# Moving the V gathers from GpSimd's queue to SyncE's, and a second buffer for attention output

## Chip, cores, metric

One core of one Trainium2 chip. The metric is device time in microseconds (us), the median of several executions. "State" says whether a run was fast or more than 1.5% above the fastest run of the same kernel (slow); verdicts use fast runs alone.

## The reference

Two branches share a layer-normalised input `xn` of 2048 tokens by 512 and are added to the input.

```python
# A: 32 heads of 16; each token looks at 8 keys, itself and those 2, 4 .. 14 tokens back
q, k, v = split(xn @ wqkv)
logits = einsum('bhsd,bhswd->bhsw', q, k_gathered) * scale     # masked where the index is < 0
o = einsum('bhsw,bhswd->bhsd', softmax(logits), v_gathered) @ wo
# B: gated MLP with mixing over tokens
z = gelu(xn @ w_in); z1 = z[:896]; z2 = layernorm(z[896:])
g = einsum('ts,bsf->btf', w_sp, z2) + b_sp                     # w_sp is 2048 x 2048
out = x + o + (z1 * g) @ w_out
```

## The kernel before

A small planner records every operation with what it reads and writes, estimates durations, fixes an order for each engine, and sets semaphore waits. For TensorE (PE) it keeps the order of the program. After projections and normalisation (to about 108 us) come four waves, tc = 0 to 3, of 512 tokens each. Each needs a transposed quarter of the spatial weights (2 MB in bf16, by transposing DMA, into one of two slots), and V rows for the attention sums, which VectorE (DVE) computes in two pairs, par = 0 and 1. I call the weight transposes wT0 to wT3 and the pairs (tc, par).

```python
def ld_wT(tc):                      # weights of wave tc; slot tc % 2; SyncE (SP)
    return dma("sp", lambda e: e.dma_start_transpose(AC(WT[tc % 2], [[512, NB], [1, 512]]),
                                                     B_w_sp[512 * tc: 512 * tc + 512, :]), ...)

def ld_V(j, par):                   # V gather: 128 rows of 9216 B from a scratch in HBM; GpSimd (POOL)
    src = bass.AP(tensor=vscr.tensor, offset=..., ap=[[1024, 128], [1, 4608]])
    dma("pool", lambda e: e.dma_start(A("Ve", 4608, 4608 * par), src), ..., writes=[("Ve", par)])

def pv_pair(j, par):                # DVE: two products of 4096, then sums a, b, c; the last into On
    ...
    return dma("sp", lambda e: e.dma_start_transpose(OT_of(j, par), A("On", 1024)), ...)  # attention transpose
# ... (cut)
for tc in range(NJ):
    # ... PE: products of the wave, with plain passes of the next one and output of the last between them
    for par in range(2):
        if tc > 0:
            ld_V(tc, par)
        sp_seq.append(pv_pair(tc, par))             # sp_seq: SP issues these in this order
        if par == 1 and tc + 2 < NJ:
            sp_seq.append(ld_wT(tc + 2))
```

Of the kernel before, what the change touches and what calls it, by code (L numbers as in the profile page):

```python
# [324 lines left out]
def build_kernel(nc, A_x, A_wqkv, A_wo, B_x, B_w_in, B_w_sp, B_b_sp, B_w_out, out, report=False, sched_kw=None,  # L325
# [3 lines left out]
    D = A_x.shape[2]  # L329
    assert D == 512 and S % 512 == 0  # L330
    NB = S // 128
    NJ = S // 512
# [5 lines left out]
    FILL = cfg["fill"]  # L338
# [8 lines left out]
    vscr = nc.dram_tensor("vscr", (2 * VPR, 512), BF).ap()  # L347
# [12 lines left out]
    off = {}  # L360
# [38 lines left out]
    with ExitStack() as es:  # L399
# [12 lines left out]
        def A(name, n, o2_=0):  # L412
            return ar[:, off[name] + o2_: off[name] + o2_ + n]
# [4 lines left out]
        def AC(o_, dims):  # L418
            return bass.AP(tensor=ar, offset=o_, ap=[[AR, 128]] + [list(d) for d in dims])
# [15 lines left out]
        def R1(key, name, n, o_=0):  # L435
            R(key, "sb", [(off[name] + o_, off[name] + o_ + n)])
# [26 lines left out]
            R1(("xn", s_), "xn", 512, 512 * s_)  # L463
            R1(("Vn", s_), "Vn", 512, 512 * s_)
        R1("Vs", "Vs", 4096)
        R1("On", "On", 1024)
        for s_ in range(2):
            R1(("Ve", s_), "Ve", 4608, 4608 * s_)
            for q in range(4):
# [47 lines left out]
        def c_dve(n, mode=1.0):  # L517
            return 155.0 + n / (0.96 * mode)
# [3 lines left out]
        def T(eng, fn, **kw):  # L522
            t = plan.add(eng, fn, **kw)
            if eng == "pe" and not t.name.startswith(("warm", "fill", "xTr", "red")):
                pe_seq.append(t)
            return t

        def dma(eng, fn, nbytes, chan, reads=(), writes=(), name="", xbar=False, prio=None):
            d = dict(chan=chan, nbytes=nbytes, xbar=xbar)
            if xbar:  # L530
                d["iss"] = 7700.0 if nbytes > 1000000 else 1200.0
            return T(eng, fn, reads=tuple(reads), writes=tuple(writes), name=name, prio=prio, dma=d)
# [9 lines left out]
          name="steps0")  # L542
        T("dve", lambda v: v.memset(FCa(foff["st6"] + 8, [[9, NB], [1, 1]]), LN_EPS * D), writes=["st_eps"], est=160,
          name="steps1")
# [4 lines left out]
          writes=["ident"], est=350, name="ident1")  # L549
# [5 lines left out]
          writes=[("KTpad", c, 0) for c in range(4)], est=200, name="ktpad", prio=2)  # L555
# [61 lines left out]
        for which, eng in ((0, "sp"), (1, "act")):  # L617
# [4 lines left out]
                name="ld%s" % ("qk"[which]))  # L622
# [329 lines left out]
        def bdiff(tc):  # L952
            T("dve", lambda v: v.tensor_tensor(bdt[:, 0:256], A("bbc", 256, 512 * tc + 256),
                                               A("bbc", 256, 512 * tc), ALU.subtract),
              reads=["bbc"], writes=["bd"], est=c_dve(256), name="bd%d" % tc)
# [73 lines left out]
        def plain_slices(tc, bank_of, cuts=(4, 4, 4, 4), fc=FC - 1):  # L1029
            r_ = tc % 2  # L1030
            st = {}

            def part(c0, c1):
                if c0 == 0:
                    st["k"] = bank_of()
                    cp(bank(st["k"]), A("bbc", 512, 512 * tc), ["bbc"], [("ps", st["k"])], 512, "gs%d_%d" % (fc, tc))
                k = st["k"]

                def mm(t):
                    last = None  # L1040
                    for sh in range(c0, c1):
                        last = t.matmul(bank(k), AC(off["z2"] + FH * sh + 128 * fc, [[1, 128]]),  # L1042
                                        AC(WT[r_] + sh * 512, [[1, 512]]), start=False, stop=(sh == NB - 1),
                                        skip_group_check=True)
                    return last
                T("pe", mm, reads=[(("z2a", "z2b", "z2c")[fc // 3], b) for b in range(c0, c1)] + [("wB", r_, q) for q in range(4)],
                  writes=[("ps", k)], est=(c1 - c0) * c_mm(512), name="gp%d_%d_%d" % (fc, tc, c0))
                if c1 < NB:
                    return
                sl = n_cb[0] % 2  # L1050
                n_cb[0] += 1
                cv = A("cb", 512, 1024 * sl)
                cp(cv, bank(k), [("ps", k)], [("cb", sl)], 512, "ge%d_%d" % (fc, tc))
                uv = AC(off["z1T"] + fc * S + 512 * tc, [[1, 512]])
                T("dve", lambda v: v.tensor_tensor(uv, cv, uv, ALU.mult), reads=[("cb", sl)], writes=[("z1T", fc, tc)],
                  est=c_dve(512, 2.0) + 30, name="up%d_%d" % (fc, tc))
            res = []
            c0 = 0
            for n in cuts:
                res.append((n, (lambda c0, n: lambda: part(c0, c0 + n))(c0, n)))  # L1060
                c0 += n
            return res
# [58 lines left out]
        def ld_V(j, par):  # L1121
            src = bass.AP(tensor=vscr.tensor, offset=vscr.offset + (VPR * par + 256 * j + 1) * 512,
                          ap=[[1024, 128], [1, 4608]])
            dma("pool", lambda e: e.dma_start(A("Ve", 4608, 4608 * par), src),  # L1124
                128 * 4608 * 2, ("Ve", par), reads=[("vscr", i) for i in range(4 * j - 1, 4 * j + 4)],
                writes=[("Ve", par)], name="ldVe%d_%d" % (j, par), prio=FILL)

        def pv_pair(j, par):
            v0 = off["Ve"] + 4608 * par
            for q in (par, par + 2):  # L1130
                b = 4 * j + q
                iv = AC(v0 + (7 + q // 2) * 512, [[-512, 8], [32, 16], [1, 32]])
                tv = iv if q >= 2 else AC(off["Vs"], [[512, 8], [32, 16], [1, 32]])
                av = AC(off["attn"] + 256 * b, [[32, 8], [0, 16], [1, 32]])
                T("dve", (lambda tv, iv, av: lambda v: v.tensor_tensor(tv, iv, av, ALU.mult))(tv, iv, av),  # L1135
                  reads=[("attn", j)] + ([("Ve", par)] if q < 2 else []),
                  writes=["Vs"] if q < 2 else [("Ve", par)], est=c_dve(4096, 2.0), name="pv%d" % b, prio=FILL)
            st_ = v0 + 512 - off["Vs"]

            def two(o_, n):  # L1140
                return AC(off["Vs"] + o_, [[st_, 2], [1, n]])
            for n, nm in ((2048, "a"), (1024, "b"), (512, "c")):
                o_ = two(0, n) if n > 512 else AC(off["On"], [[512, 2], [1, 512]])
                T("dve", (lambda o_, n: lambda v: v.tensor_tensor(o_, two(0, n), two(n, n), ALU.add))(o_, n),  # L1144
                  reads=[] if n > 512 else ["Vs", ("Ve", par)], writes=["Vs", ("Ve", par)] if n > 512 else ["On"],
                  est=c_dve(2 * n, 2.0), name="pv%s%d_%d" % (nm, j, par), prio=FILL)
            return dma("sp", lambda e: e.dma_start_transpose(AC(off["OT"] + 2048 * j + 1024 * par, [[128, 8], [1, 128]]),
                                                             A("On", 1024)),
                       128 * 1024 * 2, ("OTd", par), reads=["On"], writes=[("OT", 4 * j + par), ("OT", 4 * j + par + 2)],
                       name="OTd%d_%d" % (j, par), xbar=True)  # L1150

        n_out = [0]
# [73 lines left out]
        sp_seq = []  # L1226
# [8 lines left out]
        for tc in range(NJ):  # L1235
            if tc == 0 and P0:
                for fc in (3, 4, 5, 0, 1, 2, 6):
                    for n_, f_ in plain_slices(0, next_bank, (16,), fc):
                        f_()
                for n_, f_ in plain_slices(1, next_bank, (16,)):  # L1240
                    f_()
                for k0 in (0, 4):
                    s_sums(k0, k0 + 4, (1, 2, 4))
                    s_sums(k0, k0 + 4, (3,))
            else:
                q_ = []
                pl = plain_slices(tc + 1, ob) if tc + 1 < NJ else []
                oq = [out_slices(4 * (tc - 1) + q) for q in qord] if tc > 0 else [[], [], [], []]
                q_ = oq[0] + oq[1] + oq[2] + oq[3] + pl
                tot = sum(n for n, f in q_)  # L1250
                state = dict(done=0.0, gaps=0)

                def gap():
                    state["gaps"] += 1
                    while q_ and (state["done"] + 0.5 * q_[0][0] < tot * state["gaps"] / 9.0 or state["gaps"] == 9):
                        n, f = q_.pop(0)
                        f()
                        state["done"] += n
                for i in range(3):
                    prod7(i, tc, gap)  # L1260
                assert not q_
            for par in range(2):
                if tc > 0:
                    ld_V(tc, par)
                sp_seq.append(pv_pair(tc, par))
                if par == 1 and tc + 2 < NJ:
                    sp_seq.append(ld_wT(tc + 2))
            if tc + 1 < NJ:
                bdiff(tc + 1)
                t_sums(tc + 1)  # L1270
# [60 lines left out]
```

## Time and profile before

| | before |
|---|---|
| median of the runs known at the prediction | 259.72 us (259.46 to 263.94) |
| span of the profiled execution | 270.6 us |
| busy: PE, DVE, ACT (ScalarE), POOL | 239.3, 195.5, 142.6, 48.5 us |
| wT2, issue to landing | 47.4 us (of the four the shortest 10.1, the median 12.5) |
| V gather, issue to landing | 6.2 to 28.4 us, median 11.4 |

Landing means that a transfer's completion was signalled. The page's execution is a slow one by the rule above: its span alone is 4% above the fastest run (270.6 against 259.46 us). The waits on the page are longer than in an ordinary run. PE is the engine to watch: it is busy for 239.3 of the 270.6 us, so what costs time is what makes it idle, or halves its granted clock (0.50 from 162.4 to 169.2 us and from 172.7 to 189.6 us, 1.00 to 157.5 us). Its lines are shown in the prediction.

### The profile page before, as it was taken

To read this page: it belongs to the slowest core of one execution; us is meant where nothing else is said; L and a number is where in the kernel's file an instruction comes from. 1 tells how busy PE (TensorE), PEld (TensorE's weight loads), DVE (VectorE), ACT (ScalarE), POOL (GpSimd) and SP (SyncE) were. 2 spreads that over 40 slices of the span, in tenths; PEclk is the share of its full clock that TensorE was granted. 3 is DMA by queue.
4 is the path that set the end of the run, shared out by engine and by line. 5 is a ranking of instruction groups with operands and counts; after the bars stand their busy time and mean duration, and the time that the engine had idled before them with its cause. 6 is when DMAs were issued, how large, how long until landed. Compare 5 with 4: busy or idle time off the path is not lost.

```text
span 270.6 us, 3722 instructions
## 1 busy us (share of the span) xinstructions
PE 239.3 (88%) x1439; PEld 131.0 (48%) x1439; DVE 195.5 (72%) x228; ACT 142.6 (53%) x293; POOL 48.5 (18%) x82
## 2 busy tenths in 40 slices
PE   8999999999999999999999826005989998999994
PEld 2544434343453344444477614003767775777753
DVE  4687799899899899998994490004999999962020
ACT  2896669569899668671235303100345543545424
POOL 4648565760430400000000000000000000000000
PEclk9999999999999999999999995755999999999999
DMA  7969998320092490591099999998999663031112
GB/s 235 354 113 287 255 319 130 22 78 2 16 290 83 102 227 4 174 179 54 0 52 141 153 132 65 113 95 155 175 220 296 169 188 72 19 80 39 41 39 78
DMA packets 61697, 35.51 MB, mean 131 GB/s; under 512 B 49388, under 2 KB 60012, under 8 KB 60656
## 3 DMA queue, kind: packets, MB, share of 16 engines
q1 hardware_dynamic: 53600, 18.29, 42.5%
q0 software_dynamic: 1968, 11.55, 16.4%
q10 hardware_dynamic: 6112, 5.44, 8.9%
q8 instruction: 11, 0.18, 0.4%
q14 instruction: 6, 0.05, 0.1%
HBM read 19.01 MB, written 4.21 MB: 86 GB/s over the span
## 4 chain that ended last, share of the span: by engine, by line
PE 65%; DMA 15%; DVE 7%; SPq 6%; ACT 4%; ACTq 2%; issue 1%; POOL 0%; DVEq 0%
PE ps L1088 15%; PE ps L1042 11%; PE ps L1188 10%; PE ps L869 9%; PE ps L852 9%; DMA out_dram<-arena 8%; PE ps L729 5%; SPq L933 5%; PE ps L763 3%; PE ps L709 3%; DMA arena<-in_B_w_in_dram 2%; DMA arena<-in_B_b_sp_dram 2%; DVE arena L1135 2%; ACT arena L1015 1%; DVE arena L949 1%; DMA arena<-in_A_x_dram 1%
## 5 line engine op out<-in xcount | busy, mean ns | idle before, releaser
L1088 PE MATMUL ps<-arena 128*128 128x256 bf16 x504 | 62.6, 280 | 8.6 <-ACT ps L1015 8.6
L1088 PEld LDWEIGHTS ps<-arena 128*128 128x128 bf16 x504 | 50.5, 101 | 22.5 <-ACT ps L1015 9.9
L1144 DVE TENSOR_TENSOR arena<-arena 128x4096 bf16<-128x4096 bf16 (+2 forms) x24 | 33.6, 1401 | 31.1 <-DMA arena<-arena 30.6
L1015 ACT ACTIVATE arena<-ps 128x512 bf16<-128x512 f32 (+3 forms) x45 | 22.5, 501 | 54.2 <-PE ps L1042 19.1
L1042 PE MATMUL ps<-arena 128*128 128x512 bf16 x160 | 36.5, 385 | 16.1 <-DMA arena<-in_B_w_sp_dram 16.1
L1188 PE MATMUL ps<-arena 128*128 128x512 bf16 (+2 forms) x187 | 42.6, 371 | 1.1 <-DMA arena<-arena 1.1
L1135 DVE TENSOR_TENSOR arena<-arena 128x4096 bf16<-128x4096 bf16 x16 | 36.6, 2289 | 0.6
L755 DVE TENSOR_TENSOR arena<-arena 128x4096 bf16<-128x4096 bf16 x16 | 36.1, 2283 | 0.0
L1042 PEld LDWEIGHTS ps<-arena 128*128 128x128 bf16 x160 | 15.7, 99 | 34.8 <-issue 17.3
L729 PE MATMUL ps<-arena 128*128 128x512 bf16 x128 | 29.3, 380 | 0.0
L1188 PEld LDWEIGHTS ps<-arena 128*128 128x128 bf16 x187 | 19.6, 109 | 15.7 <-DMA arena<-arena 1.4
L852 PE MATMUL ps<-arena 128*128 128x448 bf16 x128 | 26.3, 353 | 0.4 <-DMA arena<-in_B_w_in_dram 0.3
L1124 POOL DMA_DIRECT2D arena<-vscr x8 | 4.4, 554 | 120.9 <-DVE arena L1144 118.8
L869 PE MATMUL ps<-arena 128*128 128x512 bf16 x112 | 25.0, 379 | 0.0
L1015 ACT ACTIVATE ps<-arena 128x512 f32<-128x512 bf16 (+3 forms) x36 | 19.0, 535 | 7.5 <-DMA arena<-in_A_x_dram 3.5
L737 ACT ACTIVATE arena<-ps 128x1024 bf16<-128x1024 f32 x16 | 16.3, 1019 | 7.9 <-PE ps L729 7.9
L857 ACT ACTIVATE arena<-ps 128x448 bf16<-128x448 f32 x32 | 17.2, 546 | 5.3 <-PE ps L852 3.8
L729 PEld LDWEIGHTS ps<-arena 128*128 128x128 bf16 x128 | 12.0, 98 | 16.1 <-issue 1.7
L874 ACT ACTIVATE arena<-ps 128x512 bf16<-128x512 f32 x28 | 15.8, 600 | 5.2 <-PE ps L869 5.0
L852 PEld LDWEIGHTS ps<-arena 128*128 128x128 bf16 x128 | 11.8, 98 | 13.6 <-issue 2.1
L1015 ACT ACTIVATE ps<-ps 128x256 f32<-128x256 f32 x27 | 9.9, 367 | 16.0 <-PE ps L1088 9.5
L1112 DVE TENSOR_TENSOR arena<-ps,wtt 128x512 bf16<-128x512 f32 x9 | 6.2, 687 | 15.8 <-ACT arena L1015 15.8
(67 smaller groups left out, 240.5 us busy)
## 6 DMA issues: line engine op xcount, KB each, us to landing
arena<-vscr POOLq DMA_DIRECT2D x8, 1152.0 KB, 11.4
arena<-in_A_x_dram ACTq DMA_DIRECT2D x18, 128.0 KB, 4.5
vscr<-arena POOLq DMA_DIRECT2D x16, 128.0 KB, 5.0
out_dram<-arena ACTq DMA_DIRECT2D x15, 128.0 KB, 3.0
arena<-in_A_x_dram SPq DMA_DIRECT2D x14, 128.0 KB, 6.8
arena<-in_A_wqkv_dram SPq DMA_DIRECT2D x2, 512.0 KB, 7.8
arena<-in_B_w_in_dram SPq DMA_DIRECT2D x1, 896.0 KB, 5.3
arena<-in_B_w_out_dram SPq DMA_DIRECT2D x1, 896.0 KB, 5.2
```

The source lines that it names most:

```text
L729: last = t.matmul(bank(k + which), AC(off["wqk"] + 1024 * dc + col0, [[1, 128]]), AC(off["xnT"] + dc * S + 512 * j, [[1, 512]]), start=(dc ...
L737: T("act", lambda a: a.activation(AC(qo, [[ko - qo, 2], [1, 512]]), ps[:, 512 * k: 512 * k + 1024].rearrange("p (t n) -> p t n", t=2), ACT ...
L755: T("dve", lambda v: v.tensor_tensor(pbv, qb, kb, ALU.mult), reads=rd, writes=[("pb", s_)], est=c_dve(4096, 2.0), name="prod%d_%d" % (j, c ...
L852: last = t.matmul(ps[:, 512 * k: 512 * k + HF], AC(off["xnT"] + dc * S + 128 * b, [[1, 128]]), AC(off["w_in2"] + FH * dc + c0, [[1, HF]]), ...
L857: T("act", (lambda k, hf: lambda a: a.activation(A("z2", HF, FH * b + HF * hf), ps[:, 512 * k: 512 * k + HF], ACTF.Gelu_apprx_tanh, accum_ ...
L869: lastm = t.matmul(bank(k), AC(off["w_in1"] + FH * dc + 128 * fc, [[1, 128]]), AC(off["xnT"] + dc * S + 512 * j, [[1, 512]]), start=(dc == ...
L1015: T("act", lambda a: a.activation(out_, in_, ACTF.Copy), reads=reads, writes=writes, est=c_act(n), name=name)
L1042: last = t.matmul(bank(k), AC(off["z2"] + FH * sh + 128 * fc, [[1, 128]]), AC(WT[r_] + sh * 512, [[1, 512]]), start=False, stop=(sh == NB ...
L1088: last = t.matmul(half(bk), lh(k), rh(k), start=False, stop=(k == NK - 1), skip_group_check=True)
L1135: T("dve", (lambda tv, iv, av: lambda v: v.tensor_tensor(tv, iv, av, ALU.mult))(tv, iv, av), reads=[("attn", j)] + ([("Ve", par)] if q < 2 ...
L1144: T("dve", (lambda o_, n: lambda v: v.tensor_tensor(o_, two(0, n), two(n, n), ALU.add))(o_, n), reads=[] if n > 512 else ["Vs", ("Ve", par ...
L1188: last = t.matmul(po, lh, rh, start=False, stop=(q == len(order) - 1), skip_group_check=True)
```

## The change

The intent is to take the gathers off GpSimd's software queue (q0 in the transfer tables), chain them on SyncE's hardware queue (q1) between the transposes, and let VectorE write one pair's sums while the other's transpose is still reading.

```diff
-        R1("On", "On", 1024)
+        R1(("On", 0), "On", 1024)
+        R1(("On", 1), "D", 1024)
@@ ld_V
-            dma("pool", ... name="ldVe%d_%d" % (j, par), prio=FILL)
+            return dma("sp", ... name="ldVe%d_%d" % (j, par))
@@ pv_pair
+            s_ = par if j else 0
+            on = off["D"] if s_ else off["On"]
... the last sum and its transpose use `on` and ("On", s_) instead of On
@@ waves
             for par in range(2):
-                if tc > 0:
-                    ld_V(tc, par)
                 sp_seq.append(pv_pair(tc, par))
+                if tc + 1 < NJ:
+                    sp_seq.append(ld_V(tc + 1, par))
```

More of the change, by code (lines that the diff above doesn't have):

```diff
@@ L1123, in ld_V @@
                           ap=[[1024, 128], [1, 4608]])
-            dma("pool", lambda e: e.dma_start(A("Ve", 4608, 4608 * par), src),
-                128 * 4608 * 2, ("Ve", par), reads=[("vscr", i) for i in range(4 * j - 1, 4 * j + 4)],
-                writes=[("Ve", par)], name="ldVe%d_%d" % (j, par), prio=FILL)
+            return dma("sp", lambda e: e.dma_start(A("Ve", 4608, 4608 * par), src),
+                       128 * 4608 * 2, ("Ve", par), reads=[("vscr", i) for i in range(4 * j - 1, 4 * j + 4)],
+                       writes=[("Ve", par)], name="ldVe%d_%d" % (j, par))
         def pv_pair(j, par):
             v0 = off["Ve"] + 4608 * par
+            s_ = par if j else 0
+            on = off["D"] if s_ else off["On"]
             for q in (par, par + 2):
@@ L1142, in pv_pair @@
             for n, nm in ((2048, "a"), (1024, "b"), (512, "c")):
-                o_ = two(0, n) if n > 512 else AC(off["On"], [[512, 2], [1, 512]])
+                o_ = two(0, n) if n > 512 else AC(on, [[512, 2], [1, 512]])
                 T("dve", (lambda o_, n: lambda v: v.tensor_tensor(o_, two(0, n), two(n, n), ALU.add))(o_, n),
-                  reads=[] if n > 512 else ["Vs", ("Ve", par)], writes=["Vs", ("Ve", par)] if n > 512 else ["On"],
+                  reads=[] if n > 512 else ["Vs", ("Ve", par)], writes=["Vs", ("Ve", par)] if n > 512 else [("On", s_)],
                   est=c_dve(2 * n, 2.0), name="pv%s%d_%d" % (nm, j, par), prio=FILL)
             return dma("sp", lambda e: e.dma_start_transpose(AC(off["OT"] + 2048 * j + 1024 * par, [[128, 8], [1, 128]]),
-                                                             A("On", 1024)),
-                       128 * 1024 * 2, ("OTd", par), reads=["On"], writes=[("OT", 4 * j + par), ("OT", 4 * j + par + 2)],
+                                                             AC(on, [[1, 1024]])),
+                       128 * 1024 * 2, ("OTd", par), reads=[("On", s_)], writes=[("OT", 4 * j + par), ("OT", 4 * j + par + 2)],
                        name="OTd%d_%d" % (j, par), xbar=True)
```

## The prediction

> **What bounds the kernel now.** I read the page's slices first, to see where the bounding engine falls idle, then the waits, to see what it waits for, then the timelines of the queues and the transfer table of the stretches concerned, to see why that comes late.
>
> ```profile
> PE   8999999999999999999999826005989998999994
> PEclk9999999999999999999999995755999999999999
> ```
>
> A slice is 6.77 us. TensorE (PE) is at eight or nine tenths in the first 22 slices and again in the last twelve, so it bounds the kernel everywhere except from about 150 to 190 us, where it falls idle and its granted clock drops to half. The waits name the reasons:
>
> ```profile
> DVE arena L1144 <- DMA arena<-arena: 30.6, 2, 23.4
> PE ps L1042 <- DMA arena<-in_B_w_sp_dram: 16.1, 1, 16.1
> ACT arena L1015 <- DMA out_dram<-arena: 11.1, 2, 10.6
> PE ps L1088 <- ACT ps L1015: 8.6, 3, 6.9
> ```
>
> The columns are total us, times, longest. PE waited 16.1 us for a spatial-weight transpose (the third, wT2), and 6.9 us for ACT, which itself had waited 10.6 us for an output store that had not landed. A third PE wait, 1.1 us, is for the transpose of the attention output. VectorE (DVE) waited 7.2 and 23.4 us for transposes of attention output to land, because the single buffer On can't be rewritten earlier. All three kinds are late transfers in one stretch. The timelines of SyncE (SP) and GpSimd (POOL) show what was in flight:
>
> ```profile
> 135.90 2.13 SPq L1147 DMA_TRANSPOSE arena<-arena  x1
> 138.07 44.62 SPq L933 DMA_TRANSPOSE arena<-in_B_w_sp_dram  x1
> 182.74 1.31 SPq L1147 DMA_TRANSPOSE arena<-arena  x1
> ...
> 136.18 0.55 POOL L1124 DMA_DIRECT2D arena<-vscr  x1 [21.09 <-DVE arena L1144]
> 153.63 0.53 POOL L1124 DMA_DIRECT2D arena<-vscr  x1 [16.91 <-DVE arena L1144]
> ```
>
> Columns: start, duration. SP needs 44.6 us merely to issue wT2; the first weight transpose took 7.58 us to issue. Beside wT2 run two V gathers of 1152 KB from POOL's queue; they landed after 16.2 and 28.4 us. The transfer table of two stretches (packets, MB, busy share of 16 engines), first the first weight transpose from 73 to 83 us, with no V gather beside it, then wT2 beside a gather from 165 to 179.9 us:
>
> ```profile
> DMA packets 8416, 2.62 MB, mean 262 GB/s; under 512 B 8288, under 2 KB 8288, under 8 KB 8416
> q1 hardware_dynamic: 8224, 2.10, 95.5%
> ...
> DMA packets 1658, 1.43 MB, mean 96 GB/s; under 512 B 1385, under 2 KB 1560, under 8 KB 1560
> q1 hardware_dynamic: 1351, 0.35, 77.9%
> q0 software_dynamic: 111, 0.90, 26.8%
> ```
>
> Alone, a transpose packet (2.10 MB / 8224 = 256 B) took 0.955*16*10 us / 8224 = 18.6 ns. Beside the gather it took 0.779*16*14.9 us / 1351 = 137 ns, and the total rate fell from 262 to 96 GB/s. A gather packet itself is cheap: the trace's DMA records have its 9216 B at 351 ns when nothing is mixed in, so 128 of them over 16 engines need 8*0.351 = 2.8 us. **Both** streams are slow at once, with the engines busy. So this isn't a shortage of bandwidth: the two queues disturb each other.
>
> [...] q0 and q1 advance together (the table above). [...] after 6.9 us and 16.1 us of idleness the stretch 157.5 to 191 has a mean granted clock of 0.64.
>
> **The change part by part.**
> *Queue.* The eight gathers leave POOL's queue q0 for SP's q1, ordered behind the attention-output transpose that precedes them and, for the next ones, before the weight transpose. Issue cost: 0.54 us each on POOL, about 0.6 us on SP (SP's 128 KB direct loads took 0.56 to 0.59 us), 4.8 us in all on an engine that is nearly always idle: nothing. [...] That same-queue neighbours don't hurt shows from 23 to 25 us, where the records have 256 B transposes at 18 ns in q1 beside plain loads of 1024 and 1792 B in q1, 337 GB/s together. After the change: attention-output transpose issued 135.9, gather 137.2, wT2 137.8; the gather takes 2.8 us, wT2 8192*18.6 ns/16 = 9.5 us,[...] some 2.5 us for ACT's stores and loads in q10 beside it (from 153 to 159 us wT2 beside q10 alone ran at 29 ns a packet, so 10 ns more on some 4000 packets / 16). So wT2 lands near 153 to 155 us instead of 185.5.
> *PE.* Without the 1.08 us and 6.88 us waits (the stores land in about 3 us in calm stretches) PE reaches the first matmul on wT2 at 157.5-1.1+2.6 = 159 us, where 2.6 us is the work at full clock that now lies from 164.4 to 169.5. wT2 is there by then, with some 4 us to spare. Removed: 1.08+6.88+16.06 = 24.0 us of idleness. With it goes the half clock: L1088 x16 and L1188 x4 took 3.59+1.52 against 1.75+0.86 us (2.5 us), and L1042 x4 with L1088 x24 took from 185.60 to 191.07, 5.5 us, against 0.86+2.62 (2.0 us). Sum 28.5 us.
> *Second buffer.* The sum of pair (j,1) for j>0 goes to the softmax area D, free by then. It removes the 23.4 us wait at 186.2 us directly. The first DVE wait, 7.2 us, is at j=1, par=0, still in On; it goes because its transpose is no longer mixed with a gather (landing 3 us instead of 16.7).
> *From page to time.* 270.6-28.5 = 242.1 us of span. But the page is of a bad execution: the run list has a core span of 257.4 us at clock 0.979 for a time of 259.1 us, close to the median 259.72. Check: half-clock time is 2*(1-0.956)*270.6 = 24 us in the page and 2*(1-0.979)*257.4 = 10.8 us there, so the ordinary stall is about half as long; 257.4-242.1 = 15.3 us can be removed in an ordinary run. With the 1.7 us between span and time: 242.1+1.7 = 243.8; I add 0.2 for small new waits and say **244.0 us**.
>
> **Rivals.** *A: the same 16 engines, nothing gained*[...]. Bytes don't change, so if packets of 9216 B hurt transposes from any ring the stall stays: 256 to 260 us. Against it: the two rates above[...]. *B: SP's chain holds the gathers up.* A gather may wait behind a weight transpose whose issue takes 7.6 to 10.3 us, and wT3 waits for PE to finish with the old weights, holding the next gathers. [...] Against: DVE reaches the pair (2,0) at about 156 us and its gather, behind wT2's issue, lands near 155; wT3 goes at about 166, so the gathers behind it start near 177 and DVE wants them at 183. A miss of some us in both places, passed to PE, makes 246 to 251. *C: DVE becomes the bound.* From 136 to the end DVE works 14.1+9.9+51.9 = 76 us and PE (at full clock) about 100, so no; but its order is chosen anew by the kernel's own scheduler, whose model now sees gathers on SP, and an unlucky order could cost 2 to 4 us. *D: the buffer alone does the work.* Then PE would still stand 16 us for wT2, and the time would stay above 256; the weight's lateness, not On, ends PE's wait.
>
> **Range and chances.** The floor is PE's work: busy 239.3 less 4.5 of half-clock excess, plus the 7 us of idleness at the start, the tail and small gaps, is the 242.1 of span again, so little below 242 is possible: low 241.5. Rivals B and C give the upper side: 251. A and D together get about one chance in fifteen; slower would need a new stall of over 20 us, for which I see no cause. Faster by over 2% (below 254.5): 0.93; within 2%: 0.06; slower: 0.01.
>
> **What would show it.** In the changed profile: the slices of PE without a gap near 150 to 190 us and a clock of 1.0 there; wT2's issue near 8 to 11 us and landing within 18 us; the waits for spatial weights and of DVE for attention transposes under 2 us each; the gathers in q1 with q0 left with the V writes only, and transpose packets near 20 ns. I'm wrong about the mixing if wT2 still takes over 25 us to land, and wrong about slack if PE waits for a gather's consumer (DVE waiting on vscr) by several us.

wT2's landing: from its issue 137.8 + 2.8 + 9.5 + 2.5 + 2.5 = 155.1 us. In the records of the kernel before, the first two weight transposes, with no gather beside them, took 2.9 and 1.8 us longer from issue to landing than their packets moved (11.2 against 8.3, 10.1 against 8.3).

## The result and the profile after

The changed kernel takes 244.14 us (243.27 to 246.3, 4 runs) against 261.83 us (259.46 to 268.09, 4 runs) before. The ratio is 0.9417, with a 95% interval of 0.9313 to 0.9521. Ratios here are the mean of one kernel's fast runs over the mean of the other's of the same rounds, so they aren't quite the ratios of the medians. The order of instructions on PE, DVE and ACT came out the same in both kernels; only SP's and POOL's lists differ. So the difference lies in the transfers and in what waits for them.

The slices of the changed kernel, of 6.06 us each now:

```profile
PE   7999999999999999999999999999699999999994
PEclk9999999999999999999999999999999999999999
```

PE's hole is gone, but for one slice at six tenths, and the granted clock never falls. Its waits in total, with times and the longest:

```profile
DVE arena L1138 <- DMA arena<-vscr: 3.2, 1, 3.2
...
PE ps L1089 <- ACT ps L1016: 2.5, 2, 2.0
```

PE's waits for weights (16.1 us) and attention transposes, and DVE's for attention transposes (30.6 us), no longer appear. What is left is one wait of DVE for a gather and a short one of PE. SP's timeline from the same stretch as before:

```profile
135.81 2.00 SPq L1150 DMA_TRANSPOSE arena<-arena  x1
137.85 0.58 SPq L1125 DMA_DIRECT2D arena<-vscr  x1
138.48 12.41 SPq L934 DMA_TRANSPOSE arena<-in_B_w_sp_dram  x1
150.93 1.31 SPq L1150 DMA_TRANSPOSE arena<-arena  x1
152.29 0.58 SPq L1125 DMA_DIRECT2D arena<-vscr  x1
```

wT2 took 12.4 us to issue instead of 44.6, and landed 16.7 us after its issue, at 155.2 us. In the DMA records 122 of gather (1,1)'s 128 packets began before wT2's first, at 142.5 us. The second gather, for pair (2,0), was issued behind wT2: its first packet began at 155.2 us, when wT2 had just landed, and it landed at 159.4. The transfer table from 144 to 149 us, with wT2 in flight:

```profile
DMA packets 4852, 1.34 MB, mean 268 GB/s; under 512 B 4718, under 2 KB 4852, under 8 KB 4852
...
q1 hardware_dynamic: 4702, 1.20, 112.4%
q10 hardware_dynamic: 150, 0.14, 14.6%
```

A packet of q1 took 1.124*16*5 us / 4702 = 19.1 ns, about the 18.6 ns of the first weight transpose. PE's timeline has its first matmuls on wT2 with no wait before them, and its one longer wait some 14 us later:

```profile
158.65 1.03 PE L1043 MATMUL ps<-arena 128*128 128x512 bf16 x4
...
172.81 1.92 PE L1089 MATMUL ps<-arena 128*128 128x256 bf16 x16 [2.04 <-ACT ps L1016]
```

The chain of waits leads from that wait back through ACT and DVE to the gather of pair (2,0): DVE stood 3.2 us for it, and PE lost 2.0 us in the end.

### The profile page after: what moved, and what is told of

The parts are those of the page before. It is cut to its first block, busy times and chain, and to the rows that moved or that the text cites. A ratio compares the mean times of both kernels' runs of the same rounds, so it can differ in the third digit from the quotient of the medians.

```text
span 242.4 us, 3719 instructions
## 1 busy us (share of the span) xinstructions
PE 235.1 (97%) x1439; PEld 129.7 (54%) x1439; DVE 195.4 (81%) x228; ACT 142.7 (59%) x293; POOL 44.1 (18%) x74
## 4 chain that ended last, share of the span: by engine, by line
PE 80%; DVE 13%; DMA 3%; ACT 2%; issue 1%; ACTq 1%; SPq 0%; DVEq 0%
PE ps L1089 15%; PE ps L730 12%; PE ps L1043 11%; PE ps L870 10%; PE ps L853 10%; PE ps L1191 10%; PE ps L710 6%; DVE arena L1138 6%; PE ps L764 4%; DVE arena L1147 3%; DMA arena<-vscr 3%; PE ps L633 2%; DVE arena L950 2%; ACT arena L1016 1%; DVE arena L1113 1%
## 5 line engine op out<-in xcount | busy, mean ns | idle before, releaser
L1089 PE MATMUL ps<-arena 128*128 128x256 bf16 x504 | 59.9, 273 | 2.5 <-ACT ps L1016 2.5
L1089 PEld LDWEIGHTS ps<-arena 128*128 128x128 bf16 x504 | 49.1, 98 | 14.5 <-ACT ps L1016 3.0
L1191 PE MATMUL ps<-arena 128*128 128x512 bf16 (+2 forms) x187 | 41.9, 366 | 0.0
L1191 PEld LDWEIGHTS ps<-arena 128*128 128x128 bf16 x187 | 19.5, 108 | 13.9 <-ACT ps L1016 0.2
L1043 PEld LDWEIGHTS ps<-arena 128*128 128x128 bf16 x160 | 15.7, 98 | 18.0
L730 PEld LDWEIGHTS ps<-arena 128*128 128x128 bf16 x128 | 12.0, 98 | 16.1 <-issue 1.7
L853 PEld LDWEIGHTS ps<-arena 128*128 128x128 bf16 x128 | 11.9, 98 | 13.7 <-issue 2.3
L1016 ACT ACTIVATE ps<-ps 128x256 f32<-128x256 f32 x27 | 9.9, 367 | 15.6 <-PE ps L1089 11.3
L870 PEld LDWEIGHTS ps<-arena 128*128 128x128 bf16 x112 | 10.6, 98 | 13.9 <-issue 0.8
```

Of the source, the lines that this page charges most:

```text
L730: last = t.matmul(bank(k + which), AC(off["wqk"] + 1024 * dc + col0, [[1, 128]]), AC(off["xnT"] + dc * S + 512 * j, [[1, 512]]), start=(dc ...
L853: last = t.matmul(ps[:, 512 * k: 512 * k + HF], AC(off["xnT"] + dc * S + 128 * b, [[1, 128]]), AC(off["w_in2"] + FH * dc + c0, [[1, HF]]), ...
L870: lastm = t.matmul(bank(k), AC(off["w_in1"] + FH * dc + 128 * fc, [[1, 128]]), AC(off["xnT"] + dc * S + 512 * j, [[1, 512]]), start=(dc == ...
L1016: T("act", lambda a: a.activation(out_, in_, ACTF.Copy), reads=reads, writes=writes, est=c_act(n), name=name)
L1043: last = t.matmul(bank(k), AC(off["z2"] + FH * sh + 128 * fc, [[1, 128]]), AC(WT[r_] + sh * 512, [[1, 512]]), start=False, stop=(sh == NB ...
L1089: last = t.matmul(half(bk), lh(k), rh(k), start=False, stop=(k == NK - 1), skip_group_check=True)
```

## The experiments

The theory on trial: gathers in another queue than the transposes disturb them, and moving them into the same queue cures it. The rivals: the buffer does the work; wT2 is late for another reason; the disturbance belongs to GpSimd's queue alone; the length of the packets matters. In all traces compared here the order of VectorE's and ScalarE's computing instructions is that of the kernel before.

| run | edit, in short | median us | ratio to before |
|---|---|---|---|
| e1_queue_only | changed, one buffer | 242.94 | 0.9412 |
| e2_buffer_only | changed, gathers on POOL | 266.54 | none given |
| e3_pool_apart | gathers on POOL, apart from wT2 and wT3 | 254.41 | 0.9833 |
| e4_no_gather | before, six gathers left out | 241.39 | 0.9351 |
| e5_act_queue | gathers on ACT's queue | 242.26 | 0.9295 |
| e6_gather_1kb | before, gather rows in pieces of 1024 B | 244.03 | 0.9366 |
| e7_gather_last | changed, gather behind weight transpose | 248.85 | 0.9542 |
| e9_act_late | as e5, gather (1,1) later | 245.53 | 0.9497 |
| e10_gather_4608 | before, gather rows in pieces of 4608 B | 243.92 | 0.943 |
| e11_split_fixed | changed, weight transposes in halves | 241.38 | 0.9351 |
| e12_after_again | the changed kernel | 243.34 | 0.9422 |

### The two parts, one at a time

e1 undoes the buffer:

```diff
-            s_ = par if j else 0
+            s_ = 0
```

> The changed kernel with the second buffer undone: gathers on SyncE, all attention output in On. Theory (two queues disturb each other): wT2 still lands within 18 us, the attention transpose of pair (1,0) lands near 154.6 us, about when VectorE wants On back at 155.6 us, so no new wait over 1 us: 243.5 to 246 us, the whole gain. Rival (the buffer does the work): 255 to 260 us, VectorE waiting over 10 us for an attention transpose.

Measured: 242.94 us (242.43 to 243.55), ratio 0.9412 (0.937 to 0.9454), a little under the expected range. DVE's only wait for these transfers in the profile of e1 is, from its waits:

```profile
DVE arena L1138 <- DMA arena<-vscr: 1.4, 1, 1.4
```

There is none for On. With attention transposes landing after 3.0 to 3.8 us, one buffer is free in time. The queue alone gives the whole gain, and the buffer adds nothing that shows.

e2 undoes the queue and keeps the buffer:

```diff
-            return dma("sp", lambda e: ...
+            return dma("pool", lambda e: ...            # and prio=FILL, as before
-                    sp_seq.append(ld_V(tc + 1, par))
+                    ld_V(tc + 1, par)
```

> The changed kernel with the gathers put back on GpSimd's queue, second buffer kept; the order of instructions on VectorE and ScalarE is unchanged. Theory: gathers and wT2 alternate again, wT2 needs 30 to 48 us to land, TensorE waits for it: 256 to 264 us. VectorE's wait of 23 us goes, but not TensorE's. Rival (buffer does the work): 244 to 248 us.

Measured: 266.54 us (261.91 to 275.11), against a median of 259.0. Two of its four runs count as slow; its two fast ones, 261.91 and 264.47, lie above the five fast runs of before (256.74 to 259.0). So the buffer alone gains nothing. In its profile, SP's timeline and PE's wait:

```profile
137.47 37.10 SPq L934 DMA_TRANSPOSE arena<-in_B_w_sp_dram  x1
```

```profile
PE ps L1043 <- DMA arena<-in_B_w_sp_dram: 21.7, 1, 21.7
```

With its second buffer DVE waited only 3.2 us for an attention transpose (30.6 us before), but 12.4 us for a gather. DVE, no longer held by On, released its gathers at 149.3 and 159.5 us, so that three of them, not two, met wT2. It is plausible that this makes e2 worse than before, but no run tests it.

### Is it the gathers at all?

e4 takes the kernel before and issues no gather after the first two (a wrong result):

```diff
                 if tc > 0:
-                    ld_V(tc, par)
+                    pass
```

> The kernel before without the six gathers of the later waves (the result is wrong on purpose: VectorE works on stale values; every other instruction is as before). Theory: with nothing to disturb it wT2 lands within 14 us of its issue, the stores within 4 us, and the whole gain appears without any move: 242.5 to 246 us, although SyncE's chain and the single On are as before. Rival (wT2 late for another reason, as its own 2 MB or the stores beside it): 252 to 260 us.

Measured: 241.39 us (241.34 to 241.48), ratio 0.9351 (0.9315 to 0.9387), a microsecond under the expected range. wT2, in SP's timeline:

```profile
137.97 7.84 SPq L933 DMA_TRANSPOSE arena<-in_B_w_sp_dram  x1
```

SP's chain, the single On and the stores are as before, and the stall is gone. The gathers cause it. At the same time 241.4 us is what PE needs when transfers never hold it up.

### Does the time overlap with the weight transposes suffice?

e3 leaves the gathers on POOL, but keeps them and wT2 or wT3 from being in flight together, by added waits.

```diff
+        for first, then in (("ldVe1_1", "wT2"), ("wT2", "ldVe2_0"), ("ldVe2_1", "wT3"), ("wT3", "ldVe3_0")):
+            byn[then].deps.add(byn[first])              # 'then' waits until 'first' has landed
```

> Gathers on GpSimd's queue as in e2, but wT2 and wT3 wait until the gather before them has landed, and the gather after each waits until it has landed; instruction order unchanged. Theory (only the overlap in time hurts, not the queue a gather is issued from): gather (1,1) 136.2 to about 144, wT2 144 to about 157, TensorE wants it at 157.5 to 159; gather (2,0) then lands near 163, 3 to 4 us later than in the changed kernel: 244 to 250 us, transposes at 18 to 25 ns a packet. Rival (GpSimd's queue is slow in itself): gathers take over 12 us alone and the time is 252 or more.

Measured: 254.41 us (252.68 to 258.75), ratio 0.9833 (0.9765 to 0.99): a miss, and a time that fits the rival. The separation gave only a small part of the gain. Its profile (of its one slow run, so I use it only to look at transfers) shows the gather (1,1), issued at 135.68 us, so slow that wT2, which waits for it, could only start at 147.84. Yet beside it was only the end of the attention transpose of pair (0,1), and ACT's small transfers. The transfer table from 139 to 147 us:

```profile
DMA packets 581, 1.21 MB, mean 151 GB/s; under 512 B 281, under 2 KB 478, under 8 KB 478
...
q0 software_dynamic: 116, 0.95, 28.5%
q10 hardware_dynamic: 221, 0.20, 7.3%
q1 hardware_dynamic: 244, 0.06, 3.2%
```

The three shares add up to 39%: the engines were idle most of the time with a gather unfinished, and both queues trickled. So an attention transpose beside a gather on POOL's queue is enough to slow both, here by gaps between packets and not by long packets: in the DMA records of this stretch the 103 packets of 9216 B took 353 ns on average, the 217 of 256 B took 18.

The rival, that GpSimd's queue is slow in itself, falls all the same. Once wT2 was through, gathers (2,0) and (2,1) ran with no transpose in flight (there is no line for q1), and both were over within 7.4 us. The transfer table from 163 to 171 us:

```profile
DMA packets 432, 2.49 MB, mean 311 GB/s; under 512 B 48, under 2 KB 176, under 8 KB 176
...
q0 software_dynamic: 288, 2.36, 75.1%
```

Nor do the profiles support that VectorE's work slows that queue: in the kernel before, VectorE stood idle from 162.9 to 186.2 us, and the stretch of 96 GB/s lies within that. GpSimd's own issuing took 0.53 to 0.60 us for the slow and the quick gathers of the later waves alike.

### Is any second queue bad?

e5 issues the gathers from ACT, which has a hardware queue of its own (q10).

```diff
+        for t in [t for t in plan.order["pool"] if t.name.startswith("ldVe")]:
+            plan.order["pool"].remove(t); t.eng = "act"     # then inserted in ACT's order by planned start
```

> The changed kernel with the gathers issued from ScalarE, a second hardware queue; VectorE's order unchanged, the gathers inserted in ScalarE's order by the kernel's own model of time. Theory (any second queue whose large packets alternate with transpose packets disturbs): wT2 takes over 25 us to land, transpose packets average over 50 ns beside a gather, 253 to 265 us. Rival (it is peculiar to GpSimd's software queue): wT2 within 18 us, 244 to 249 us.

Measured: 242.26 us (241.01 to 243.02), ratio 0.9295 (0.9235 to 0.9355). The rival holds in kind; its sizes were missed, as the time is below its 244 us and wT2 landed after 19.9 us where it said 18. SP's timeline:

```profile
137.67 12.27 SPq L934 DMA_TRANSPOSE arena<-in_B_w_sp_dram  x1
```

The whole gain is there with gathers and transposes in two queues. My form of the theory, any other queue, falls, unless e5 escaped because its gather was over before wT2 began moving (in the DMA records gather (1,1) ends at 142.5 us and wT2 begins at 143.1). e9 tests this: gather (1,1) goes after ACT's first output store, at 143.35 us, with wT2 under way.

```diff
+        ao.remove(g)                                        # g: the gather (1,1)
+        ao.insert([t.name.startswith("st") for t in ao].index(True) + 1, g)
```

> As e5 (gathers from ScalarE's hardware queue), but gather (1,1) is issued some 5 us after wT2, in the middle of it, where in e5 it was first. Theory (mixing with large packets from any other queue slows both; e5 escaped since the gather was over before wT2 began): gather (1,1) lands after more than 12 us, wT2 after more than 20 us, 248 to 258 us. Rival (only GpSimd's software queue with packets of 9216 B does it, a hardware queue doesn't): the gather takes its 3 to 5 us of transfer with the transposes held meanwhile, wT2 lands within 16 us, VectorE waits 3 to 5 us for the gather, 243 to 247 us.

Measured: 245.53 us (245.25 to 246.65), ratio 0.9497 (0.943 to 0.9565). wT2 landed within 13.2 us (the longest of the four). DVE waited 5.4 us for the gather. Of the mixture this isn't quite what I wanted: in the DMA records neither the store nor the gather moved data before about 147 to 148 us, when wT2 was almost through, so that the gather did not alternate with it. But two gathers then ran beside the attention transpose of (1,0). The transfer table from 148.5 to 153.5 us:

```profile
DMA packets 658, 2.11 MB, mean 423 GB/s; under 512 B 322, under 2 KB 450, under 8 KB 450
...
q10 hardware_dynamic: 368, 2.05, 101.2%
q1 hardware_dynamic: 290, 0.07, 6.9%
```

Beside attention transposes again, as in e3, but 423 GB/s in place of 151. In the records of this stretch both queues advance 48 packets a microsecond for some time, one of 9216 B for one of 256 B, at 350 and 18 ns. The mixture that e9 was to bring is in e5 itself, at its next gather: (2,0) moved from 151.0 to 156.8 us and met the last 357 of wT2's 8192 packets. The transfer table of e5 from 151 to 155.5 us:

```profile
DMA packets 655, 1.35 MB, mean 300 GB/s; under 512 B 402, under 2 KB 533, under 8 KB 533
...
q10 hardware_dynamic: 273, 1.26, 101.1%
q1 hardware_dynamic: 382, 0.09, 12.8%
```

From 151.5 to 153.5 us the records have 49 packets of each kind, one for one, and the gather was through in 5.8 us, against 21.9 us for the one beside wT2 in the kernel before (159.6 to 181.5 us). The transposes are held back meanwhile, but the gather isn't. So in e5 and e9 packets of this length alternated with transposes without harm to the gather.

### Does the length of the packets matter on GpSimd's queue?

e6 and e10 are the kernel before with nothing changed but the shape of the gather's rows: nine pieces of 1024 B, which the records show as packets of 4096 B, or two of 4608 B. The pieces are also written in reverse, a precaution of mine against their being joined to one row again; no run shows whether it was needed, so cutting and reversing are not told apart.

```diff
-  ap=[[1024, 128], [1, 4608]]                    -> A("Ve", 4608, 4608 * par)
+  ap=[[1024, 128], [-512, 9], [1, 512]]          # e6, from the last piece back, both sides
+  ap=[[1024, 128], [-2304, 2], [1, 2304]]        # e10
```

> The kernel before with each gather cut into 1024 B pieces (nine times the packets, same bytes[...]). Theory [...] wT2 lands within 25 us and the time falls to 245 to 253 us. Rival (what counts is the total gather time in the other queue, 1152 packets of 46 ns as against 128 of 351): wT2 over 35 us and 256 to 264 us.

> The kernel before with each gather row in two pieces of 4608 B, on GpSimd's queue (e6 had nine pieces of 1024 B, which the records show as packets of 4096 B). If the length of the packet that a transpose meets matters in proportion: about halfway, 248 to 254 us, wT2 landing in 20 to 30 us. If 4608 B is already short enough or any cutting cures it: 242.5 to 246 us as e6. If only packets up to 4096 B are harmless: 256 to 264 us as before.

Measured: e6 244.03 us (243.54 to 244.33), ratio 0.9366 (0.9324 to 0.9408); e10 243.92 us (243.25 to 249.48), ratio 0.943 (0.936 to 0.9499). Both give the whole gain with the gathers still on POOL, e6 even a little more than its theory expected. wT2 landed after 17.7 and 16.9 us. There is no halfway: a packet half as long does not do half the harm, it does none that shows. The transfer tables with gather and transposes in flight, e6 from 138 to 143.5 us:

```profile
DMA packets 1075, 1.37 MB, mean 249 GB/s; under 512 B 787, under 2 KB 787, under 8 KB 1075
...
q0 software_dynamic: 304, 1.18, 69.9%
q1 hardware_dynamic: 771, 0.19, 26.7%
```

and e10 from 142.5 to 147.5 us (the profile is of its slow run, whose early part came some 5 us late):

```profile
DMA packets 1264, 1.41 MB, mean 283 GB/s; under 512 B 1011, under 2 KB 1011, under 8 KB 1264
...
q0 software_dynamic: 268, 1.17, 63.7%
q1 hardware_dynamic: 996, 0.25, 49.4%
```

In both the gather passes within 5.0 us (138.3 to 143.2 us in e6, 143.5 to 148.1 in e10) while the transposes are held back, then wT2 goes on. In the kernel before both crawled. Its profile had already shown short packets of GpSimd's queue beside a weight transpose without harm: within the prediction's window from 73 to 83 us that queue wrote V, 128 packets of 4096 B from 80.6 us on, beside the end of the first weight transpose, which landed after 11.2 us.

### The order in SyncE's chain

e7 puts gather (1,1) behind wT2, and (2,1) behind wT3.

```diff
+            so[ig], so[iw] = so[iw], so[ig]                 # in SP's order
```

> The changed kernel with gather (1,1) issued behind wT2, and (2,1) behind wT3, on the same queue. Theory: one ring, so no disturbance whichever comes first: wT2 lands within 16 us, but gather (1,1) lands near 154 us instead of 144, and VectorE, which wants it at 146.2, waits some 7 to 8 us; half of it or more reaches TensorE through the products: 247 to 252 us. Rival (being ahead of wT2 is what protects it, disturbance in either order otherwise): wT2 over 25 us, 255 or more.

Measured: 248.85 us (247.58 to 249.03), ratio 0.9542 (0.9489 to 0.9595). No transpose of the weights took over 11.3 us to land. The waits:

```profile
DVE arena L1138 <- DMA arena<-vscr: 5.5, 1, 5.5
PE ps L1089 <- ACT ps L1016: 4.4, 1, 4.4
```

As expected: with the queue shared, wT2 stays quick in either order (at most 11.3 us to land here, 16.7 in the changed kernel, 47.4 before), and a late gather costs PE most of what it costs DVE (4.4 of 5.5 us). The chain's order is worth about 5 us (248.85 against 244.14 and 243.34 of the changed kernel).

### A faster version

The last wait of the changed kernel comes from gather (2,0) standing behind wT2. I cut wT2 and wT3 in halves and put the gather between them. The first try, e8_split_wT, was faulty: the plain passes were entered before the second half in program order, so that the half waited for them and they read old weights. It passed the comparison with the reference, presumably because that part contributes little. Its 257.34 us says nothing.

> An attempt to beat the changed kernel: wT2 and wT3 in two halves, the gather of pair (2,0) or (3,0) between them on SyncE's queue. Gather (2,0) should land near 152 instead of 159.4 us, VectorE's 3.2 us wait and most of TensorE's 2.5 us go: 241.5 to 243.5 us. If TensorE is the bound already and the waits only move: 243.5 to 245.

e11 enters both halves in time:

```diff
-                    sp_seq.append(ld_wT(tc + 2))
+                    sp_seq.append(ld_wTh(tc + 2, 0))
+                    half2 = ld_wTh(tc + 2, 1)               # entered now, issued later
...              after the gather of the next wave's first pair:
+                    sp_seq.append(half2)
```

> e8 mended (in e8 the plain passes were entered before the second half of the weights in program order, so that the second half waited for them and they read old weights; its numbers say nothing). Now gather (2,0) goes between the halves and should land near 152 us, so VectorE's wait of 3.2 us and TensorE's of 2.0 us go: 241.5 to 243.5 us, 0.5 to 1 us below the changed kernel of the same call. If the waits only move: no difference.

> The changed kernel itself, for the comparison with e11 on one chip: 243 to 245 us.

Measured in five rounds: e11 241.38 us (240.99 to 242.88), the changed kernel 243.34 us (243.01 to 244.35). The ranges don't overlap, and the fast runs' ratios to before, 0.9351 and 0.9422, stand as 0.9925: 0.75% faster. SP's timeline and PE's slices of e11:

```profile
147.29 0.58 SPq L1134 DMA_DIRECT2D arena<-vscr  x1
147.91 8.78 SPq L943 DMA_TRANSPOSE arena<-in_B_w_sp_dram  x1
```

```profile
PE   7899999999999999999999999999999999999994
```

The gather goes 5 us earlier than at 152.29, and PE has no dent left. This equals e4 (241.39 us), which has no gathers to wait for, so by these runs nothing more is to be had from these transfers.

## Why the prediction was right, and where it wasn't

**The bound, the stall and the time: right.** 244.0 us was predicted and 244.14 measured. PE reached its first matmul on wT2 at 158.65 us (159 predicted), wT2 landed at 155.2 (153 to 155), the clock stayed at 1.0, and PE's busy time fell by 4.2 us from that of the slow page (4.5 predicted for the half clock). e4 confirms that the gathers alone made the stall, and e2 that the weight's lateness, not On, held PE.

**Two terms of the sum were off and cancelled, which is luck.** I took 242.1 us of span as the floor; e4 and e11 have 239.7 and 239.6, so some 2.4 us more could be removed than I counted. I counted 0.2 us for small new waits; PE had 2.5 us of waits for ACT. The first error lies in counting only the three large waits: PE's two short ones after the stall, 0.74 and 0.98 us, also went in e11. The rest of the 2.4 us I can't assign.

**"It removes the 23.4 us wait at 186.2 us directly": true, but not needed.** With the buffer alone (e2) DVE's waits for attention transposes fall to 3.2 us, and the kernel gains nothing. e1 has one buffer and no such wait either. It came from an attention transpose stuck behind wT2 in SP's chain, and once wT2 is quick it doesn't arise. No part of the predicted time rested on it.

**"The two queues disturb each other": right in direction, wrong in its cause.** It led to the right time, since sharing one queue (242.94 us in e1) is one of several cures. But e5 and e9 have another queue and 9216 B packets without the harm (wT2 landed after 19.9 and 13.2 us), and e10 has half the packet on the same queue and none of it (16.9 us). What the runs show in its place: in them the harm needs the uncut 9216 B rows, GpSimd's queue, and transposes in flight, all three. With the rows cut (e6 244.03 us, e10 243.92), or on ScalarE's (e5, 242.26) or SyncE's queue (the change, 244.14), the gain is there; without a transpose in flight (e3 from 163 to 171 us) the uncut rows pass quickly on GpSimd's queue, at 311 GB/s. Why these three together make both streams trickle isn't settled, nor where between 4608 and 9216 B it begins. A gather on ScalarE's queue was seen beside attention transposes (e9) and the tail of a weight transpose (e5), not beside a whole one.

Some readings that led there don't hold. "With the engines busy": in the records from 165 to 179.9 us the median transpose packet still took 18 ns and the median gather packet 354; a minority of long ones, up to 0.76 and 5.1 us, make the mean. At the median times all packets of that stretch would fill about 28% of the engines' time (an estimate from these records), so packets stood still rather than moved. "Alone", and 262 GB/s: that window holds 0.52 MB of V writes and the transfer's end; while only transposes moved, from 74 to 80.5 us, the records give 281 GB/s. ScalarE's gathers made 423 with attention transposes beside them in e9, so these plain transfers were the faster ones. And from 23 to 25 us `prof` gives 330 GB/s, not 337.

**Rivals.** A fell, with the note that its premise was true: the bytes and the engines are the same, and the time still changed by 6%. B occurred in small: gather (2,0) landed at 159.4 us, not near 155, since wT2 itself needed 12.4 us to issue behind gather (1,1) (8 to 11 predicted), whose packets took 4.4 us to pass and not 2.8; DVE waited 3.2 us and PE 2.0. e7 makes B large, e11 removes it. C didn't occur, as the orders came out identical. D fell by e1 and e2.

## What to carry to other kernels

When two transfers are both slow while the engines that carry them have time to spare, look at which queues and packet lengths meet, before counting bytes: here cutting a 9216 B row in two on the same queue was worth as much as moving the gathers (243.92 us in e10, 244.14 with the move). Test the parts of a change one at a time; the plausible second buffer did nothing. And once transfers share one queue, their order is the next thing to tune: e7's order cost some 5 us, and a long transfer cut in two let the urgent one through and gave the last 0.75% (241.38 against 243.34 us).
